# Float64 weights rounded in other steps, a piece apart, and mostly beside the first batch's MLP

## The chip, the cores and the metric

The kernel runs on one core of a Trainium2 chip. The metric is device time in microseconds (us) of one execution. Executions of one kernel agree within about 0.3%. The engines are named as the profile names them: PE (TensorE, matrix products), PEld (its weight loads), DVE (VectorE), ACT (ScalarE), POOL (GpSimd), SP (SyncE, which only issues transfers here).

## The reference, cut to what matters

```python
# attention: 8 batches, 12 heads, 448 positions, 64 per head, float32
q_n, k_n = rmsnorm(q, g_q), rmsnorm(k, g_k)
attn = softmax(q_n @ k_n.T / 8)
x = (attn @ v)  # (8, 12, 448, 64), rearranged to 3584 tokens x 768
# MLP: the weights w_in (768 x 2048) and w_out (2048 x 768) come as float64
h = x @ w_in
out = ((h - np.tanh(h)) @ w_out).astype(np.float32)
```

The weights arrive as float64. The kernel loads them as pairs of 32-bit words (low and high) and builds float32 values from them. This building is called rounding here. It works on 64 pieces of 128 partitions x 384 values, 32 for w_in and 32 for w_out.

## The kernel before: the parts that matter

The work is cut into slots, one for each pair of heads, 48 in all. In slot s the kernel loads for s+3, normalises and transposes for s+2, computes scores and exponentials for s+1, and the product with v for s. Between these parts lie four gaps, in which pieces of the previous batch's MLP and roundings are emitted. In the traces below an engine that waits for one instruction holds up those emitted after it.

```python
def round_weight(nc, pool, raw, dst, n):          # all of one piece at once
    lo, hi = raw[:, :, 0], raw[:, :, 1]
    ...
    nc.vector.tensor_scalar(out=ex, in0=hi, scalar1=0x7FF00000, ..., op0=ALU.bitwise_and)        # exponent
    nc.gpsimd.tensor_scalar(out=exf, in0=ex, scalar1=8.0, scalar2=-896.0 * 2**23, op0=ALU.mult, op1=ALU.add)
    nc.gpsimd.tensor_scalar(out=ex, in0=exf, scalar1=255.0 * 2**23, scalar2=0.0, op0=ALU.min, op1=ALU.max)
    nc.vector.tensor_scalar(out=man, in0=hi, ..., op0=ALU.bitwise_and, op1=ALU.bitwise_or)       # mantissa
    nc.vector.scalar_tensor_tensor(out=manf, in0=lo.bitcast(U32), scalar=2.0**-32, in1=man, ...)
    nc.vector.scalar_tensor_tensor(out=ex, in0=hi, scalar=-(2**31), in1=ex, ...)                 # sign
    nc.scalar.mul(manf, manf, 2.0**-20)
    nc.gpsimd.tensor_tensor(out=dst, in0=manf, in1=exf, op=ALU.mult)

# slot(s):  norm(s+2): squares (POOL), sums (DVE), pow (POOL), n = q * rr (DVE)
#           scores(s+1, 0); gap(0); values(s): av, dn (PE), rd = 1/dn and xT = av*rd (DVE); gap(1)
#           scores(s+1, 1); gap(2); turn(s+2): transposes (PE), kT (DVE), qT (ACT); gap(3)
for s in range(-2, NP + NP // 2):                 # NP = 6 slots a batch
    # slots -2..5: 32 pieces of w_in, no MLP; slots 6..8: 32 pieces of w_out beside the first MLP
    ...
    weight(n + 3, n)                              # load 3 ahead into 3 raw buffers, round
```

The hidden layer of the MLP accumulates in two PSUM tiles: `th` (tanh, ACT) and `gT` (h - th, DVE) must have read a tile before PE can fill it again.

## Time and profile before

| | before |
|---|---|
| time, median of the runs with the changed kernel | 1763.6 us |
| stage 1: slots 0 to 4, attention only, a slot | 23.4 us |
| the same, mean of slots 0 to 5 by their first scores: (190.9 - 46.5) / 6 | 24.1 us |
| stage 2: slots 6, 7 and 8, first MLP begins | 42.9, 50.6, 51.0 us |
| from slot 9 on, PE always busy, a slot | 32.55 us |

A slot's time runs from the start of its product with v (av) to that of the next. Where one time is given for all of stage 1, it is the mean of six slots between first scores, as in the second row.

Busy times by stage, from the table of windows. The columns are: window and its length in us; busy us (and instructions) of PE, PEld, DVE, ACT and POOL; granted PE clock; DMA share; GB/s.

```profile
29.80:194.60 164.80, 89.69 (x361) 37.22 (x359) 106.37 (x163) 47.63 (x92) 96.76 (x106) 0.71 0.33 97
194.60:346.30 151.70, 118.80 (x346) 53.78 (x347) 113.09 (x175) 36.37 (x72) 83.47 (x104) 0.90 0.33 95
346.30:1759.00 1412.70, 1407.38 (x4792) 709.81 (x4792) 473.28 (x558) 261.95 (x482) 194.31 (x122) 1.00 0.09 26
```

The third line is PE-bound: 1407 of 1413 us busy at full clock. The first two are not bound by any one engine. These 316 us are where a change to the rounding can act. The first two lines begin at 29.8 and 194.6 us: the first scores of slot 0 came at 46.5 us and those of slot 6 at 190.9.

### The profile page before, as it was taken

How to read it: one execution, taken by the hardware profiler on the slowest of the kernel's cores; microseconds unless marked ns; L12 is line 12 of the kernel's file. 1: busy time of each engine (PE TensorE's matmuls, PEld its weight loads, DVE VectorE, ACT ScalarE, POOL GpSimd, SP SyncE). 2: the span in 40 equal slices, each digit the busy share in tenths (PEclk: the TensorE clock that was granted, in tenths of full speed). 3: DMA queues.
4: the chain of work that ended last, by engine and by line, in shares of the span. 5: the costliest groups of instructions: out<-in, count | busy, mean ns of one | idle time of the engine just before them, and what ended most of it. 6: DMA issues, size and time to landing. Idle time of an engine off the chain costs nothing.

```text
span 1759.5 us, 14368 instructions
## 1 busy us (share of the span) xinstructions
PE 1621.6 (92%) x5512; PEld 804.2 (46%) x5512; DVE 705.2 (40%) x923; ACT 351.2 (20%) x653; POOL 388.9 (22%) x350
## 2 busy tenths in 40 slices
PE   1566767899999999999999999999999999999998
PEld 1222333355445554455445554454455544455555
DVE  4666777743443333433442333332442333421100
ACT  1232222212121122112121122112221112210100
POOL 5565555521112112112111112111121111100000
PEclk9776888999999999999999999999999999999999
DMA  4333332301001101011001110010001110000000
GB/s 119 103 91 102 90 100 83 93 29 40 22 16 40 35 25 27 21 34 35 21 16 40 35 35 16 26 40 26 21 16 40 35 36 16 10 14 9 0 19 20
DMA packets 93585, 70.23 MB, mean 40 GB/s; under 512 B 48452, under 2 KB 89412, under 8 KB 93508
## 3 DMA queue, kind: packets, MB, share of 16 engines
q1 hardware_dynamic: 93184, 69.23, 13.6%
q8 instruction: 45, 0.74, 0.2%
q14 instruction: 32, 0.26, 0.0%
q10 hardware_dynamic: 324, 0.00, 0.0%
HBM read 58.20 MB, written 11.01 MB: 39 GB/s over the span
## 4 chain that ended last, share of the span: by engine, by line
PE 80%; POOL 8%; DVE 8%; issue 2%; ACT 1%; DMA 0%; SPq 0%; POOLq 0%; ACTq 0%; DVEq 0%
PE mm L286 34%; PE mm L259 29%; PE sc L199 7%; PE av L228 7%; POOL w_exp L47 2%; POOL rr L161 2%; DVE w_exp L56 2%; POOL w_exp L44 2%; PE dn L237 2%; DVE rd L242 1%; POOL n L157 1%; DVE rr L158 1%; POOL w_out L60 1%; PE sc L177 1%; PE sc L182 1%
## 5 line engine op out<-in xcount | busy, mean ns | idle before, releaser
L259 PE MATMUL mm<-xT,w_in 128*128 128x448 f32 x1536 | 609.7, 551 | 20.7 <-DVE gT L266 20.6
L286 PE MATMUL mm<-w_out,gT 128*128 128x384 f32 x1536 | 513.6, 490 | 0.0
L259 PEld LDWEIGHTS mm<-xT,w_in 128*128 128x128 f32 x1536 | 289.1, 193 | 325.9 <-issue 315.3
L286 PEld LDWEIGHTS mm<-w_out,gT 128*128 128x128 f32 x1536 | 286.1, 190 | 222.4 <-issue 36.8
L204 ACT ACTIVATE p<-sc,rr 112x448 f32<-112x448 f32 x384 | 212.4, 633 | 382.7 <-PE sc L199 382.6
L242 DVE RECIPROCAL rd<-dn 128x448 f32<-128x448 f32 x48 | 141.9, 2955 | 249.6 <-PE dn L237 249.6
L157 POOL TENSOR_TENSOR n<-k_nat 112x512 f32<-112x512 f32 x48 | 49.9, 1039 | 765.5 <-PE sc L182 758.2
L199 PE MATMUL sc<-qT,kT 64*112 64x448 f32 x768 | 183.6, 599 | 33.0 <-DVE kT L179 33.0
L228 PE MATMUL av<-p,v_nat 112*64 112x448 f32 x768 | 159.7, 559 | 0.0
L266 DVE TENSOR_TENSOR gT<-mm,th 128x448 f32<-128x448 f32 x128 | 79.5, 621 | 200.0 <-ACT th L265 200.0
L265 ACT ACTIVATE th<-mm 128x448 f32<-128x448 f32 x128 | 69.6, 544 | 448.5 <-PE mm L259 433.1
L218 DVE TENSOR_TENSOR sum<-p 112x896 f32<-112x896 f32 x84 | 91.7, 1092 | 151.9 <-ACT p L204 147.5
L161 POOL TENSOR_TENSOR rr<-rr,neg_half 112x16 f32<-112x16 f32 x48 | 139.3, 2902 | 50.7 <-DVE rr L160 49.6
L199 PEld LDWEIGHTS sc<-qT,kT 64*112 64x112 f32 x768 | 66.6, 184 | 130.8 <-issue 91.6
L158 DVE TENSOR_REDUCE rr<-n 112x8 f32<-112x512 f32 x96 | 65.6, 683 | 92.9 <-POOL n L157 92.9
L228 PEld LDWEIGHTS av<-p,v_nat 112*64 112x64 f32 x768 | 52.2, 141 | 103.4 <-issue 102.3
L177 PE MATMUL sc<-ident,k_nat 112*128 112x112 f32 x192 | 30.1, 284 | 71.6 <-ACT p L204 63.1
L164 DVE TENSOR_TENSOR n<-q_nat,rr 112x512 f32<-112x512 f32 x48 | 36.4, 759 | 147.0 <-POOL rr L161 147.0
L286 PE MATMUL mm<-w_out,g_rest 128*128 128x384 f32 x256 | 85.4, 489 | 0.0
L157 POOL TENSOR_TENSOR n<-q_nat 112x512 f32<-112x512 f32 x48 | 49.9, 1039 | 141.0 <-DVE rr L158 141.0
L59 ACT ACTIVATE w_man<-w_man 128x384 f32<-128x384 f32 x64 | 33.4, 522 | 218.7 <-DVE w_man L53 218.6
L177 PEld LDWEIGHTS sc<-ident,k_nat 112*128 112x128 f32 x192 | 24.0, 153 | 92.5 <-ACT p L204 70.4
(37 smaller groups left out, 679.7 us busy)
## 6 DMA issues: line engine op xcount, KB each, us to landing
w_raw<-in_moe_w_in_dram SPq DMA_DIRECT2D x32, 384.0 KB, 3.4
w_raw<-in_moe_w_out_dram SPq DMA_DIRECT2D x32, 384.0 KB, 3.1
k_nat<-in_k_dram SPq DMA_DIRECT2D x96, 112.0 KB, 3.1
q_nat<-in_q_dram SPq DMA_DIRECT2D x48, 224.0 KB, 3.1
v_nat<-in_v_dram SPq DMA_DIRECT2D x48, 224.0 KB, 2.6
out_dram<-o_sb SPq DMA_DIRECT2D x48, 192.0 KB, 1.9
out_dram<-o_sb SPq DMA_DIRECT2D x16, 96.0 KB, 2.2
gcol<-in_g_q_dram ACTq DMA_DIRECT2D x2, 0.2 KB, 2.3
```

Of the source, the lines that this page charges most:

```text
L157: nc.gpsimd.tensor_tensor(out=sq, in0=rows, in1=rows, op=ALU.mult)
L158: nc.vector.reduce_sum(rr[:, i], sq, axis=AX.X)
L161: nc.gpsimd.tensor_tensor(out=rr2, in0=rr2, in1=neg_half, op=ALU.pow)
L177: nc.tensor.transpose(tk[:, c * CP : (c + 1) * CP], kn[:, c].rearrange("p h d -> p (h d)"), ident[:CP, :CP])
L199: nc.tensor.matmul(sc[:CP, :S], lhsT=kT[r, c * CP : (c + 1) * CP], rhs=qT[r, :], start=True, stop=True)
L204: nc.scalar.activation(p[:, h, i, :], tiles[h][:CP, :S], AF.Exp, scale=rr[:, 0, 2 * c + h : 2 * c + h + 1])
L218: nc.vector.tensor_tensor(out=u, in0=a, in1=z, op=ALU.add)
L228: nc.tensor.matmul(av[h * D : (h + 1) * D, :S], lhsT=v_nat[:, h, c, :], rhs=p[:, h, c % 2, :], start=(c == 0), stop=(c == NCH - 1),)
L242: nc.vector.reciprocal(rd, dn[:, :S])
L259: nc.tensor.matmul(hps[:, :S], lhsT=w_in_sb[f][:, c, :], rhs=xT[b, c], start=(c == 0), stop=(c == CD - 1))
L266: nc.vector.tensor_tensor(out=g[:, f, :], in0=hps[:, :S], in1=th, op=ALU.subtract)
L286: nc.tensor.matmul(ops[:, :HALF], lhsT=lhs[:, f, :], rhs=w_out_sb[f][:, d], start=(f == 0), stop=(f == CF - 1),)
```

## The change

The intent: fewer steps for a piece, no engine that waits inside a piece (the second half of a piece is emitted after the first half of the next), and less rounding ahead of the first MLP. The raw words of w_in are loaded into the memory that later holds w_out, so up to 14 can be loaded ahead. n moves behind rd and xT on DVE, kT from DVE to ACT.

The new steps of a piece: ACT scales the absolute value of the high word, read as a float, and scales the low word; POOL limits the first of these to a range (called the clamp here). Then DVE shifts the bits into place and puts the sign back, and POOL adds the low word's share to the bits.

```diff
+HI_MIN, HI_MAX = 2.0**-31, 1.875 - 2.0**-23
+def round_weight_a(nc, raw, dst):
+    lo, hi = raw[:, :, 0], raw[:, :, 1]
+    nc.scalar.activation(dst, hi.bitcast(F32), AF.Abs, scale=2.0**-16)
+    nc.scalar.mul(lo, lo.bitcast(U32), 2.0**-29)
+    nc.gpsimd.tensor_scalar(out=dst, in0=dst, scalar1=HI_MIN, scalar2=HI_MAX, op0=ALU.max, op1=ALU.min)
+def round_weight_b(nc, raw, dst):
+    lo, hi = raw[:, :, 0], raw[:, :, 1]
+    bits = dst.bitcast(I32)
+    nc.vector.tensor_scalar(out=bits, in0=bits, scalar1=4, scalar2=1, op0=ALU.logical_shift_left, op1=ALU.logical_shift_right)
+    nc.vector.scalar_tensor_tensor(out=bits, in0=hi, scalar=-(2**31), in1=bits, op0=ALU.bitwise_and, op1=ALU.bitwise_or)
+    nc.gpsimd.tensor_tensor(out=bits, in0=bits, in1=lo, op=ALU.add)
...
+    EARLY = 20
+        if n < 2 * CF:                       # w_in: staged where w_out will be
+            raw = w_out_sb[n % CF].bitcast(I32).rearrange("p (f w) -> p f w", w=2)
...
+        else:                                # w_out: three raw buffers, as before
+            raw = wp.tile([P, HALF, 2], I32, name="w_raw")
...
+    def weight(to):
+        for n in range(done[1], min(to, 4 * CF)):
+            round_weight_a(nc, raws[n], weight_dst(n)[2])
+            if n:
+                round_weight_b(nc, raws.pop(n - 1), weight_dst(n - 1)[2])
+            done[1] = n + 1
+            while done[0] < min(max(min(n + 14, 2 * CF + 3), n + 3), 4 * CF):
+                weight_load(done[0])
+                done[0] += 1
...
-        nc.vector.tensor_scalar(out=kT, in0=tk[:, :S], scalar1=g_col, ...)
+        nc.scalar.mul(kT, tk[:, :S], g_col)
...
         for f in range(CF):                  # hidden layer of batch 0: pieces 20 to 47
+            if b == 0:
+                weight(EARLY + (3 * CF - EARLY) * (f + 1) // CF)
...
+                if b == 0 and n == 0:        # first column half of its output: pieces 48 to 63
+                    weight(3 * CF + CF * (t * CF + f + 1) // (FULL * CF))
...
         gap(1)
+        if has(2):
+            norm_q(s + 2)                    # n, here in place of the end of norm
...
+    for s in range(-2, NP):                  # 20 pieces in slots -2 to 5
+        slot(s, lambda j: weight(EARLY * (4 * (s + 2) + j + 1) // (4 * (NP + 2))))
```

More of the change, by code (lines that the diff above doesn't have):

```diff
@@ L60, in round_weight @@
     nc.gpsimd.tensor_tensor(out=dst, in0=manf, in1=exf, op=ALU.mult)
+HI_MIN, HI_MAX = 2.0**-31, 1.875 - 2.0**-23
[7 more added lines that the diff above has]
+    bits = dst.bitcast(I32)
+    nc.vector.tensor_scalar(
+        out=bits, in0=bits, scalar1=4, scalar2=1, op0=ALU.logical_shift_left, op1=ALU.logical_shift_right
+    )
+    nc.vector.scalar_tensor_tensor(
+        out=bits, in0=hi, scalar=-(2**31), in1=bits, op0=ALU.bitwise_and, op1=ALU.bitwise_or
+    )
+    nc.gpsimd.tensor_tensor(out=bits, in0=bits, in1=lo, op=ALU.add)
 def bounded_path(tc, ctx, q, k, v, moe_w_in, moe_w_out, out, g_col, ident, ones, neg_half):
@@ L94, in bounded_path @@
     gp = pool("gp", bufs=1)
+    op = pool("op", bufs=3)
+    wp_stack = ctx.enter_context(ExitStack())
+    wp = wp_stack.enter_context(tc.tile_pool(name="wp", bufs=3))
     ps_s = pool("ps_s", bufs=4, space=PSUM)
@@ L122, in bounded_path, with weight_dst, weight_load @@
     raws = {}
-    def weight_load(wp, n):
-        f, i = n // 2 % CF, n % 2
-        raw = raws[n] = wp.tile([P, HALF, 2], I32, name="w_raw", bufs=3)
+    def weight_dst(n):
         if n < 2 * CF:
+            f, i = n // 2, n % 2
+            return f, i, w_in_sb[f].rearrange("p c f -> p (c f)")[:, i * HALF : (i + 1) * HALF]
+        i, f = (n - 2 * CF) // CF, n % CF
+        return f, i, w_out_sb[f][:, i * HALF : (i + 1) * HALF]
+    def weight_load(n):
+        f, i, _ = weight_dst(n)
+        if n < 2 * CF:
+            raw = w_out_sb[n % CF].bitcast(I32).rearrange("p (f w) -> p f w", w=2)
             rows = w_in_words[i * HALF : (i + 1) * HALF, f * 2 * P : (f + 1) * 2 * P]
@@ L138, in weight_load @@
             )
-    def weight_round(wp, n):
-        f, i = n // 2 % CF, n % 2
-        if n < 2 * CF:
-            dst = w_in_sb[f].rearrange("p c f -> p (c f)")[:, i * HALF : (i + 1) * HALF]
-        else:
-            dst = w_out_sb[f][:, i * HALF : (i + 1) * HALF]
-        round_weight(nc, wp, raws.pop(n), dst, HALF)
+        raws[n] = raw
+    done = [0, 0]
+    def weight(to):
[7 more added lines that the diff above has]
+                done[0] += 1
+        if done[1] == 4 * CF and raws:
+            round_weight_b(nc, raws.pop(4 * CF - 1), weight_dst(4 * CF - 1)[2])
     normed, turned, probs, sums, xT = {}, {}, {}, {}, {}
@@ L161, in norm, with norm_q @@
         nc.gpsimd.tensor_tensor(out=rr2, in0=rr2, in1=neg_half, op=ALU.pow)
+        normed[s] = rr
+    def norm_q(s):
+        rr = normed[s]
         t = loaded.pop(("q", s))
@@ L178, in turn @@
         kT = qkp.tile([P, S], F32, name="kT")
-        nc.vector.tensor_scalar(out=kT, in0=tk[:, :S], scalar1=g_col, scalar2=None, op0=ALU.mult)
+        nc.scalar.mul(kT, tk[:, :S], g_col)
         tq = ps_s.tile([P, 512], F32, name="sc")
@@ L270, in hidden @@
         late["g"] = g
-    def project(b):
-        op = late["op"]
-        g = late.pop("g")
-        if b % 2 == 0:
-            late["rest"] = op.tile([P, CF, P], F32, name="g_rest", bufs=1)
-        o = (b % 2) * REST
-        nc.gpsimd.tensor_copy(out=late["rest"][:, :, o : o + REST], in_=g[:, :, FULL * P :])
-        for t in range(FULL + b % 2):
-            lhs = g[:, :, t * P : (t + 1) * P] if t < FULL else late["rest"]
-            for n in range(2):
-                d = slice(n * HALF, (n + 1) * HALF)
-                ops = ps_m.tile([P, 512], F32, name="mm")
-                for f in range(CF):
-                    nc.tensor.matmul(
-                        ops[:, :HALF], lhsT=lhs[:, f, :], rhs=w_out_sb[f][:, d],
-                        start=(f == 0), stop=(f == CF - 1),
-                    )
-                    if f < CF - 1:
-                        yield 4 * HALF / ENGINE_NS
-                o_sb = op.tile([P, HALF], F32, name="o_sb", bufs=3)
-                if n == 0:
-                    nc.scalar.copy(out=o_sb, in_=ops[:, :HALF])
-                else:
-                    nc.vector.tensor_copy(out=o_sb, in_=ops[:, :HALF])
-                if t < FULL:
-                    r0 = b * S + t * P
-                    nc.sync.dma_start(out=out[r0 : r0 + P, d], in_=o_sb)
-                else:
-                    for i in range(2):
-                        r0 = (b - 1 + i) * S + FULL * P
-                        nc.sync.dma_start(out=out[r0 : r0 + REST, d], in_=o_sb[i * REST : (i + 1) * REST])
-                yield 4 * HALF / ENGINE_NS
@@ new lines, in rest @@
+    def rest(b):
+        if b == 0:
+            late["op"] = pool("late", bufs=1)
+        if b % 2 == 0:
+            late["rest"] = late["op"].tile([P, CF, P], F32, name="g_rest")
+        o = (b % 2) * REST
+        nc.gpsimd.tensor_copy(out=late["rest"][:, :, o : o + REST], in_=late["g"][:, :, FULL * P :])
+    def project(b):
+        g = late["g"]
+        units = [(t, n) for t in range(FULL + b % 2) for n in range(2)]
+        if b == 0:
+            units.sort(key=lambda u: u[1])
+        else:
+            rest(b)
+        for t, n in units:
+            lhs = g[:, :, t * P : (t + 1) * P] if t < FULL else late["rest"]
+            d = slice(n * HALF, (n + 1) * HALF)
+            if b == 0 and (t, n) == (0, 1):
+                wp_stack.close()
+                rest(b)
+            ops = ps_m.tile([P, 512], F32, name="mm")
+            for f in range(CF):
+                if b == 0 and n == 0:
+                    weight(3 * CF + CF * (t * CF + f + 1) // (FULL * CF))
+                nc.tensor.matmul(
+                    ops[:, :HALF], lhsT=lhs[:, f, :], rhs=w_out_sb[f][:, d],
+                    start=(f == 0), stop=(f == CF - 1),
+                )
+                if f < CF - 1:
+                    yield 4 * HALF / ENGINE_NS
+            o_sb = op.tile([P, HALF], F32, name="o_sb")
+            if n == 0:
+                nc.scalar.copy(out=o_sb, in_=ops[:, :HALF])
+            else:
+                nc.vector.tensor_copy(out=o_sb, in_=ops[:, :HALF])
+            if t < FULL:
+                r0 = b * S + t * P
+                nc.sync.dma_start(out=out[r0 : r0 + P, d], in_=o_sb)
+            else:
+                for i in range(2):
+                    r0 = (b - 1 + i) * S + FULL * P
+                    nc.sync.dma_start(out=out[r0 : r0 + REST, d], in_=o_sb[i * REST : (i + 1) * REST])
+            yield 4 * HALF / ENGINE_NS
@@ L347, in slot @@
         gap(3)
-    with tc.tile_pool(name="wp", bufs=2) as wp:
-        done = [0, 0]
-        def weight(n_load, n_round):
-            while done[0] < min(n_load, 4 * CF):
-                weight_load(wp, done[0])
-                done[0] += 1
-                while done[1] < min(n_round, done[0] - 2):
-                    weight_round(wp, done[1])
-                    done[1] += 1
-            while done[1] < min(n_round, done[0]):
-                weight_round(wp, done[1])
-                done[1] += 1
-        load(0, "kqv")
-        weight(3, 0)
-        for s in range(-2, NP + NP // 2):
-            def gap(j, s=s):
-                if s < NP:
-                    n = 2 * CF * (4 * (s + 2) + j + 1) // (4 * (NP + 2))
-                else:
-                    n = 2 * CF + 2 * CF * (4 * (s - NP) + j + 1) // (2 * NP)
-                    run(per_slot / 4)
-                weight(n + 3, n)
-            slot(s, gap)
-    late["op"] = pool("op", bufs=3)
-    for s in range(NP + NP // 2, NS):
+    load(0, "kqv")
+    for n in range(4):
+        weight_load(n)
+    done[0] = 4
+    for s in range(-2, NP):
+        slot(s, lambda j: weight(EARLY * (4 * (s + 2) + j + 1) // (4 * (NP + 2))))
+    for s in range(NP, NS):
         slot(s, lambda j: run(per_slot / 4))
```

## The prediction

> **What bounds the kernel now.** I read the forty slices of the page first, then busy times by stage, then the timeline of one slot of each stage, then the waits of the stage that held most.
>
> ```profile
> PE   1566767899999999999999999999999999999998
> PEclk9776888999999999999999999999999999999999
> ```
>
> From slice 9 on (one slice is 44 us) PE is full at full clock; nothing the change does to VectorE, ScalarE or GpSimd can shorten that part. The time to win is in the first eight slices. The kernel works in slots of one head pair: slots -2 to 5 hold attention of the first batch and round w_in (32 pieces, 4 a slot); slots 6 to 8 start that batch's MLP and round w_out (32 pieces, 10.7 a slot); from slot 9 no rounding is left. One window of each kind:
>
> ```profile
> 97.00:120.40 23.40, 13.62 (x58) 5.56 (x56) 15.23 (x23) 6.82 (x14) 13.84 (x16) 0.72 0.33 98
> 243.60:295.80 52.20, 38.85 (x115) 16.97 (x116) 38.81 (x60) 12.74 (x27) 29.31 (x38) 0.90 0.34 97
> 378.80:411.35 32.55, 32.55 (x121) 17.18 (x122) 10.83 (x12) 5.90 (x11) 4.98 (x3) 1.00 0.13 40
> ```
>
> Columns: window, length, then busy us of PE, weight load, DVE, ACT, POOL, granted clock, DMA share, GB/s. A slot takes 23.4 us in stage 1, 52.2 in stage 2 and 32.55 where PE is the bound. No engine is full in the first two: DVE reaches 15.2 of 23.4 and 38.8 of 52.2. So it is a chain across engines, not a busy engine. The timeline of one piece in stage 2 shows it:
>
> ```profile
> 256.98 0.35 DVE L43 TENSOR_SCALAR w_exp<-w_raw 128x384 int32<-128x384 int32 x1
> 257.22 1.00 POOL L60 TENSOR_TENSOR w_out<-w_man,w_exp 128x384 f32<-128x384 f32 x1 [0.74 <-DVE w_exp L56]
> 257.25 1.18 DVE L50 TENSOR_SCALAR w_man<-w_raw 128x384 int32<-128x384 int32 x1
> 258.30 0.51 POOL L44 TENSOR_SCALAR w_exp<-w_exp 128x384 f32<-128x384 int32 x1
> 258.46 0.75 DVE L53 SCALAR_TENSOR_TENSOR w_man<-w_raw,w_man 128x384 f32<-128x384 uint32 x1
> 258.89 0.69 POOL L47 TENSOR_SCALAR w_exp<-w_exp 128x384 int32<-128x384 f32 x1
> 259.31 0.52 ACT L59 ACTIVATE w_man<-w_man 128x384 f32<-128x384 f32 x1 [2.58 <-DVE w_man L53]
> 259.61 0.56 DVE L56 SCALAR_TENSOR_TENSOR w_exp<-w_raw,w_exp 128x384 int32<-128x384 int32 x1 [0.40 <-POOL w_exp L47]
> ```
>
> DVE and POOL hand one piece to and fro, and it costs DVE 3.1 us (L43 to the next L43), which is 33 us for 10.7 pieces. Other DVE work is about 13.3 us in such a slot (rd 2.95, xT 0.96, four sums 3.4, two reductions 1.4, n 0.7, kT 0.7, 5.3 gT of 0.6), and n waits for POOL's pow and the reductions for POOL (some 6 us). 33 + 13 + 6 = 52: the slot's length. PE then waits for the tanh result to leave PSUM, behind that queue:
>
> ```profile
> PE mm L259 <- DVE gT L266: 20.6, 6, 6.3
> ```
>
> (waits of stage 2: total us, times, longest). Stage 1 has the same chain with the norm (POOL square, DVE sum, twice; pow; n) inside it.
>
> **What the Trainium skill says.**
> "SBUF — State Buffer", section Who interferes with whom: a DVE instruction in a two-port mode and a GpSimd instruction exclude each other for their whole length. The trace agrees for the tensor_scalar (L50 takes 0.35 us alone, 1.18 when it meets L60's 1.00). The page says so of two-input DVE operations too; L53 over L47 above is only slowed (0.75 against 0.56), so I count the first as a block and the second not.
> "TensorE: Matmul & The Clock Gate", section What's actually happening: after an idle window of about 3.4 us the clock is halved until a busy one. The trace: eight score matmuls take 1.76 us warm, but 3.33 at 285.7 us behind an idle gap of only 2.72.
> "ScalarE: Activation LUTs", section What ACT_TABLE_LOAD costs: 186 ns + 0.833 ns per element with immediates, 506 ns at 384; L59 takes 522.
> "GPSIMD Engine Reference", section 4.1 Engine selection: an add with all operands of one 32-bit integer type is exact there. It gives no time for it; I take L60's 1.00 us, also two inputs of 384.
>
> **The change, part by part.**
> Rounding. Before, a piece costs DVE 0.41 + 0.71 + 0.74 + 0.56 = 2.42 us, POOL 0.53 + 0.68 + 1.00 = 2.21, ACT 0.52 (mean durations of its rows). After: ACT two activations, 1.04; POOL one tensor_scalar (0.51) and one add (1.00), 1.51; DVE one tensor_scalar (0.35) and one two-input operation (0.56, issued 0.3 apart), about 0.8 alone and, with a wait behind a running POOL operation, 1.5 estimated in dense stretches. As the second half belongs to the piece before, no engine waits inside a piece.
> Placement. Stage 1 rounds 20 pieces (2.5 a slot) in place of 32; stage 2 rounds 28 (9.3 a slot) in place of 32; the last 16 go beside the first output units of slots 9 and 10, which need only the other column half. No piece comes late: output f of the hidden layer needs 2(f+1) pieces and 20 + 1.75(f+1) are rounded.
> Staging in w_out's place gives 14 loads of lookahead. It removes waits of the DMA queue, which cost nothing now, and makes a burst of 10 loads at 11 us.
> norm_q: n goes behind rd and xT on DVE, so DVE no longer sits 3 us behind pow, but n is then chained to PE. kT (0.68) goes from DVE to ACT.
>
> Stage 1 after. The rounding leaves the chain and a new loop sets the slot: scores half 0, av and dn on PE, rd and xT on DVE, n, transposes of q, qT on ACT, next scores. Warm: 1.76 + 3.2 + 3.1 = 8.0 (PE), 0.1, rd and xT 3.77 (start of L242 to the next DVE start), 0.4 for a piece in half of the slots, n 0.7, transposes 0.6, qT 0.53, handovers 0.2: 14.3 us. With the PE cold at its start, as now (scores 3.33, av 4.65, transposes 1.0), 17.6. PE's longest idle gap in it is about 2.8 us, where it sits seven now: sometimes cold, I take 16.5. POOL's own chain (last add, two squares, pow) ends about 10 us after the n before, so it is not the bound. ACT (8 exponentials 5.1, kT and qT 1.2, rounding 2.6) is at 9. The two first slots have no values; the norm chain of 7.7 us (8.55 to 16.2 in the trace) plus transposes and copies puts the first scores of slot 0 at about 27.5 us. Slot 6's scores then start at 27.5 + 6 x 16.5 = 126.5 us; before, at 190.9. Gain 64.4.
>
> Stage 2 after. DVE: 12.6 + 9.3 x 1.5 + some 3 of waits for the norm = 29.6 of 32.55; POOL 5.0 + 14.1 = 19; ACT 8 exponentials, 5.3 tanh, copies and 9.7 of rounding = 19. PE becomes the bound again, but DVE is close behind and the output of the hidden layer has only two PSUM buffers, so PE will lose a few us when gT stands behind rd and a piece. I put the slot at 36. First scores of slot 6 to its av take 10.8 now and stay; av of slot 9 comes 10.8 + 3 x 36 = 118.8 us after them, now 155.4 (346.3 - 190.9). Gain 36.6.
>
> Slots 9 and 10 carry 16 pieces, without tanh and gT: some 2 us lost. From there all is as before.
>
> Sum: 1762.8 - 64.4 - 36.6 + 2 = 1664 us, 5.6% less.
>
> **Rivals.**
> DVE stays the bound of stage 2. Its 29.6 of 32.55 rests on my 1.5 us a piece; if the port lock makes it 2.4 (0.51 + 0.35 + 0.56 + 1.00, fully in turn), the slot is 12.6 + 22 + 3, about 39 with PE's idle gaps, and the time 1674. For it: L50's 1.18. Against it: L53 overlaps.
> The loop of stage 1 keeps PE warm or cold throughout: 14.3 gives 1651, 17.6 gives 1671. For cold: the 2.72 us gap. For warm: the gap is less than half of today's.
> The burst of loads holds back k and q of the third head pair. The present highest, 119 GB/s at 0.43 share, puts the limit at an estimated 277 GB/s; 7.3 MB are queued ahead, 26 us, so they land about 32 us, just as needed. A miss costs 2 to 5 us, once.
> The rounding is hidden anyway: then nothing changes. Stage 2's 52 against 32.55 us speaks against it.
> PE stalls of stage 2 vanish: 32.55 a slot, 1654.
>
> **Range and chances.** The rivals that look likely span 1642 to 1690 when two come together. Even one stage's gain alone (36 us) passes 2% (35 us), so slower is all but excluded.
>
> **What would show it.** Slots of stage 1 at 14 to 18 us between starts of rd, with rd released by dn, and n directly behind xT. The first hidden matmul (L259 now, at 194.2 us) at about 130. Slots 6 to 8 at 33 to 39 us with PE's waits for gT under 4 us a slot. Steady slots still 32.55. The rounding's DVE tensor_scalar between 0.35 and 1.2 us. I am wrong if the integer add or the strided activation takes far over 1.00 or 0.52 us, if ACT, now with kT and two activations a piece, holds back exponentials, or if PE waits for weights at a batch's start.

## The result, and the profile after

The changed kernel takes 1690.05 us (1688.23 to 1690.59), the kernel before 1763.6. The ratio is 0.9583, 95% interval 0.9566 to 0.96. All ratios here are the mean time of one kernel's fast runs over that of the other's of the same rounds, so they aren't quite the ratio of the quoted medians. The kernel is 4.2% faster, where 5.6% was predicted. The time lies 26 us above the predicted one and just outside the range, whose end was 1690.

The forty slices of the page, now of 42 us each:

```profile
PE   5788988899999999999999999999999999999998
PEclk9788999899999999999999999999999999999999
```

PE is full from the ninth slice on in both kernels (now from about 337 us, before from about 352 us), and fuller than before in each of the first seven. In the eighth slice (295 to 337 us) PE shows an 8 still; the surprise lies close to there. The stages, in the same columns as before, with slots 9 and 10 as a stage of their own:

```profile
30.00:131.30 101.30, 79.15 (x336) 30.53 (x336) 55.83 (x69) 47.20 (x92) 70.95 (x49) 0.80 0.46 123
131.30:253.00 121.70, 111.85 (x352) 51.27 (x352) 82.38 (x108) 53.33 (x109) 92.22 (x69) 0.97 0.23 66
253.00:338.20 85.20, 72.19 (x239) 36.27 (x238) 48.95 (x59) 27.32 (x55) 58.60 (x43) 0.92 0.36 103
```

The windows start at the first scores of slot 0, the first scores of slot 6, and av of slots 9 and 11. Set beside the prediction:

| | predicted | measured | off |
|---|---|---|---|
| first scores of slot 6 | 126.5 us | 131.3 | +4.8 |
| from there to av of slot 9 | 118.8 | 121.7 | +2.9 |
| slots 9 and 10 beyond 2 x 32.55 | 2 | 20.1 | +18.1 |

The sum of the last column is 25.8 us; the profiled run (1688.2 us) lies 24 above the prediction, so these terms hold the whole miss. One term carries most of it: the two slots in which the last 16 pieces are rounded. Of its 20.1 us PE sat idle for 13.0 (85.20 - 72.19); the other 7.1 are matmuls that took longer, the granted clock being 0.92 over these slots. DVE lost its load there as intended. Beside PE, POOL is the busy one: 92 of 122 us in stage 2 and 59 of 85 in stage 3.

Stage 1, from the chain that ended last (start, us, what; the view leaves out the shortest pieces). This is one turn of the predicted loop, from scores to scores:

```profile
97.25 3.33 PE sc L251 x8
100.58 3.92 PE av L280 x16
104.50 3.03 PE dn L289 x16
107.56 2.97 DVE rd L294
110.55 0.96 DVE xT L296
112.20 0.69 DVE n L216
113.03 0.99 PE sc L234 x4
114.69 3.33 PE sc L251 x8
```

The eight score matmuls take 3.33 us: the granted clock is 0.50 there, and at 1.00 they take 1.76. rd starts when dn is done, n comes behind xT, and the transposes of q follow at once. A slot takes (131.3 - 30.4) / 6 = 16.8 us; 16.5 was predicted.

Now the clamp of the changed kernel (L74, the tensor_scalar on POOL) by its own line; the three times are the shortest, the median and the longest in ns:

```profile
L74 POOL TENSOR_SCALAR w_in<-w_in x32: 1482/1493/1862, 15.0 to 185.0; 128x384 f32<-128x384 f32 x32
L74 POOL TENSOR_SCALAR w_out<-w_out x32: 1482/1491/1919, 187.6 to 314.8; 128x384 f32<-128x384 f32 x32
```

The prediction gave it 0.51 us. Its shortest is 1.48, and the 16 that ran with no DVE instruction beside them took 1.49 too. So it isn't held up by DVE: it is that long by itself. What this does in slot 9 is seen in the timeline (start, us, engine, line, tiles, and in brackets how long the engine sat idle before, and for what):

```profile
281.78 1.06 POOL L87 TENSOR_TENSOR w_out<-w_out,w_raw 128x384 int32<-128x384 int32 x1 [1.57 <-DVE w_out L84]
...
285.92 0.55 ACT L72 ACTIVATE w_out<-w_raw 128x384 f32<-128x384 f32 x1 [4.42 <-DMA w_raw<-in_moe_w_out_dram]
286.38 0.53 ACT L73 ACTIVATE w_raw<-w_raw 128x384 int32<-128x384 uint32 x1
286.56 1.49 POOL L74 TENSOR_SCALAR w_out<-w_out 128x384 f32<-128x384 f32 x1 [0.98 <-ACT w_out L72]
286.81 0.62 ACT L231 ACTIVATE kT<-sc,g_col 128x448 f32<-128x448 f32 x1
287.32 0.52 ACT L238 COPY qT<-sc 128x448 f32<-128x448 f32 x1
287.90 1.76 PE L251 MATMUL sc<-qT,kT 64*112 64x448 f32 x8 [3.19 <-ACT qT L238]
```

ACT sat idle for 4.42 us, waiting for raw words that had not landed. kT and qT were ready to run behind it (their transposes were done at 276.8 us), but ACT keeps its order, and PE then stood 3.19 us for qT. The load was late because one of the three raw buffers is free only when POOL's add (L87) of three pieces before has read it: that add, the first line here, ended at 282.84, the load was issued at 282.87 and landed at 285.90. The waits of the changed kernel from 130 to 335 us (total us, times, longest):

```profile
ACT w_out L72 <- DMA w_raw<-in_moe_w_out_dram: 72.8, 25, 8.0
...
PE mm L353 <- POOL w_out L87: 6.6, 5, 2.9
PE mm L313 <- DVE gT L320: 6.0, 2, 3.4
PE sc L251 <- ACT qT L238: 5.3, 3, 3.2
PE sc L229 <- ACT p L256: 3.9, 2, 3.2
```

PE waits for the weight itself, for qT and for the exponentials p. Only 6.0 us are the wait for gT that ruled before (20.6).

Two theories follow. Theory A: POOL's clamp is the cause, 1 us too long on 64 pieces. Theory B: the ring of three raw buffers (add, load, two activations, clamp, add) is the cause, and a faster clamp would only shift the wait. A third question is whether stage 1 is really bound by the loop shown.

### The profile page after: what moved, and what is told of

Its sections match the earlier page's. It is cut to its first block, busy times and chain, and to the rows that moved or that the text cites. A ratio compares the mean times of both kernels' runs of the same rounds, so it can differ in the third digit from the quotient of the medians.

```text
span 1686.4 us, 14244 instructions
## 1 busy us (share of the span) xinstructions
PE 1615.3 (96%) x5512; PEld 798.6 (47%) x5512; DVE 616.1 (37%) x747; ACT 405.3 (24%) x765; POOL 415.4 (25%) x286
## 3 DMA queue, kind: packets, MB, share of 16 engines
q1 hardware_dynamic: 93184, 69.23, 14.5%
## 4 chain that ended last, share of the span: by engine, by line
PE 85%; POOL 6%; DVE 4%; issue 3%; DMA 1%; ACT 1%; SPq 0%; ACTq 0%; POOLq 0%; DVEq 0%
PE mm L353 33%; PE mm L313 31%; PE sc L251 9%; PE av L280 8%; PE dn L289 3%; POOL w_out L74 2%; DVE rd L294 2%; POOL w_out L87 1%; PE sc L234 1%; POOL n L205 1%; DMA w_raw<-in_moe_w_out_dram 1%; PE sc L229 1%; POOL rr L209 1%; POOL w_in L87 1%; POOL w_in L74 1%
## 5 line engine op out<-in xcount | busy, mean ns | idle before, releaser
L313 PE MATMUL mm<-xT,w_in 128*128 128x448 f32 x1536 | 601.7, 545 | 7.7 <-DVE gT L320 6.0
L353 PE MATMUL mm<-w_out,gT 128*128 128x384 f32 x1536 | 519.9, 494 | 6.6 <-POOL w_out L87 6.6
L313 PEld LDWEIGHTS mm<-xT,w_in 128*128 128x128 f32 x1536 | 285.7, 190 | 307.5 <-issue 293.6
L353 PEld LDWEIGHTS mm<-w_out,gT 128*128 128x128 f32 x1536 | 287.7, 191 | 233.3 <-issue 38.7
L205 POOL TENSOR_TENSOR n<-k_nat 112x512 f32<-112x512 f32 x48 | 49.9, 1040 | 736.1 <-PE sc L234 729.2
L205 POOL TENSOR_TENSOR n<-q_nat 112x512 f32<-112x512 f32 x48 | 50.0, 1041 | 139.1 <-DVE rr L206 139.1
L363 DVE COPY o_sb<-mm 128x384 f32<-128x384 f32 x28 | 15.5, 554 | 153.2 <-PE mm L353 152.9
L353 PEld LDWEIGHTS mm<-w_out,g_rest 128*128 128x128 f32 x256 | 47.9, 190 | 35.6 <-issue 4.1
L333 POOL COPY g_rest<-gT 128x1024 f32<-128x1024 f32 x8 | 9.0, 1131 | 202.2 <-DVE gT L320 202.1
L361 ACT COPY o_sb<-mm 128x384 f32<-128x384 f32 x28 | 13.4, 478 | 188.2 <-PE mm L353 188.1
```

What stands on the lines that cost most here:

```text
L205: nc.gpsimd.tensor_tensor(out=sq, in0=rows, in1=rows, op=ALU.mult)
L313: nc.tensor.matmul(hps[:, :S], lhsT=w_in_sb[f][:, c, :], rhs=xT[b, c], start=(c == 0), stop=(c == CD - 1))
L353: nc.tensor.matmul(ops[:, :HALF], lhsT=lhs[:, f, :], rhs=w_out_sb[f][:, d], start=(f == 0), stop=(f == CF - 1),)
```

## The experiments

Each edit is to the changed kernel. All results were correct.

### The clamp's two operations swapped

```diff
-    ...(out=dst, in0=dst, scalar1=HI_MIN, scalar2=HI_MAX, op0=ALU.max, op1=ALU.min)
+    ...(out=dst, in0=dst, scalar1=HI_MAX, scalar2=HI_MIN, op0=ALU.min, op1=ALU.max)
```

> The clamp on GpSimd with its two operations in the other order (min, then max; the same values). The changed kernel's clamp takes 1.49 us at its median, where I had 0.51 from the old kernel's two tensor_scalars; one of those was min then max. Theory A (it is the order of the two operations that costs): the clamp falls to 0.5 to 0.7 us, slots 9 and 10 from 42.6 to 36 or less, the time from 1690 to 1665 to 1675. Theory B (float32 in and float32 out costs 1.49 us whatever the order): clamp and time unchanged, 1690 within 3.

Measured: 1666.4 us (ratio to before 0.945, interval 0.9434 to 0.9466). The clamp's line:

```profile
L74 POOL TENSOR_SCALAR w_out<-w_out x32: 502/507/1302, 181.9 to 296.6; 128x384 f32<-128x384 f32 x32
```

The same values in the other order take 0.51 us in place of 1.49, and the kernel gains 23.6 us. Slots 6 and 7 run at 33.0 and 32.7 us, PE's own pace. Slot 10 falls to 32.5. But slots 8 and 9 still take 38.5 each, where 36 or less was expected, and ACT's wait for loads is 59 us. So the clamp is a cause, and not the only one.

### The clamp on DVE

```diff
-    nc.gpsimd.tensor_scalar(out=dst, in0=dst, scalar1=HI_MIN, ...)
+    nc.vector.tensor_scalar(out=dst, in0=dst, scalar1=HI_MIN, ...)
```

> The clamp goes from GpSimd to VectorE, so GpSimd has only the integer add of about 1.0 us a piece and VectorE one tensor_scalar more, 0.35 us alone and 1.2 behind a GpSimd operation. If GpSimd's 1.49 us is what makes slots 9 and 10 long (42.6 us against the steady 32.6), they fall to 33 to 37 and the time to 1665 to 1675. If the three staging buffers set it (load 3.1 us, two activations 1.0, the rest), they stay at 40 or more and the time at 1683 or more.

Measured: 1680.1 us (0.952), between the two cases. Slots 6 and 7 take 32.7, but slots 8 to 10 take 38.6, 43.2 and 40.5, nearly as long as with the slow clamp on POOL (39.8, 42.6 and 42.6). The clamp itself is short (0.39 us mean), but now stands in DVE's queue behind rd and xT, and POOL's adds waited 55 us for DVE's second operation on w_out pieces, where it was 7 us:

```profile
POOL w_out L87 <- DVE w_out L84: 55.3, 20, 5.3
```

So POOL was freed, but a turn of the ring was not shortened, and slots 9 and 10 stayed above 40. This speaks for theory B there, but does not prove it, as the edit also loads DVE.

### Four raw buffers

```diff
-    op = pool("op", bufs=3)
+    op = pool("op", bufs=2)
-    ...tc.tile_pool(name="wp", bufs=3)
+    ...tc.tile_pool(name="wp", bufs=4)
-            while done[0] < min(max(min(n + 14, 2 * CF + 3), n + 3), 4 * CF):
+            while done[0] < min(max(min(n + 14, 2 * CF + 4), n + 4), 4 * CF):
```

> Four raw buffers in place of three and one load more ahead (the output staging goes from three buffers to two to make room, which should cost nothing). If the ring of three buffers is the bound of slots 9 and 10 (GpSimd frees a buffer, the load takes 3.1 us, ScalarE waits for it in order), these fall from 42.6 to about 37 us and the time to about 1680; ScalarE's wait for the w_out loads falls from 73 us to under 35. If GpSimd's busy time is the bound, all stay within 3 us of 1690, with the wait moved elsewhere.

Measured: 1678.66 us (0.9522), 11.4 us less than the changed kernel, with the slow clamp in place. ACT's wait for loads fell to 50.1 us, not to 35, and slots 8 to 10 take 37.3, 34.4 and 42.3. The ring is a part of the cause; with POOL this slow the wait came back in slot 10. (The edit also takes one of three buffers from the output's staging; no run separates this.)

### Swapped clamp and four raw buffers

> The clamp as min then max (0.5 us) and four raw buffers. With the clamp swapped alone the time was 1666.4 and slots 8 and 9 still took 38.5 us each, with ScalarE waiting 59 us for w_out loads. If the ring of buffers is what is left there, both fall to 33 to 35, the wait for loads to under 35 us, and the time to 1655 to 1661. If something else holds them (the add of GpSimd behind VectorE), the time stays within 3 of 1666.

Measured: 1654.96 us (0.9391, interval 0.9375 to 0.9406). Slot 9 of the changed kernel first, for comparison, then slot 9 of this one, then its wait for loads, in the columns of the earlier views:

```profile
253.00:295.60 42.60, 34.97 (x121) 17.97 (x120) 27.61 (x33) 14.56 (x30) 33.10 (x25) 0.96 0.46 127
```

```profile
240.20:272.80 32.60, 32.60 (x121) 17.21 (x120) 26.71 (x31) 16.50 (x34) 22.96 (x26) 1.00 0.61 166
```

```profile
ACT w_out L72 <- DMA w_raw<-in_moe_w_out_dram: 27.4, 15, 6.2
```

PE is busy for all of slot 9, and slots 6 to 10 all take 32.5 to 33.2 us. Clamp and ring together account for the whole excess there, and they add up: 23.6 + 11.4 = 35.0, and 1690.05 - 1654.96 = 35.1.

### n before rd and xT in the first slots

```diff
         if has(2):
             norm(s + 2)
+            if s < NP:
+                norm_q(s + 2)
...
-        if has(2):
+        if has(2) and s >= NP:
             norm_q(s + 2)
```

> In the first slots (up to 5) n is computed before rd and xT again, as in the kernel before; later slots keep the new order. Theory: stage 1's slot of 16.8 us is the loop scores, av, dn, rd, xT, n, transposes, qT; without rd and xT in it PE and ScalarE set the slot at 12.5 to 14.5 us and the time falls by 14 to 25, to 1665 to 1676. Rival (GpSimd's norm chain or ScalarE sets it): slots stay above 16 us and the time within 4 of 1690.

Measured: 1689.84 us (0.9582), no change; the slot is (128.7 - 30.7) / 6 = 16.3 us. Stage 1 ended 2.6 us earlier, and slot 6 took 41.5 us in place of 37.5. The rival held. The timeline shows what took the loop's place:

```profile
77.42 2.94 DVE L294 RECIPROCAL rd<-dn 128x448 f32<-128x448 f32 x1
...
81.59 0.56 DVE L84 SCALAR_TENSOR_TENSOR w_in<-w_out,w_in 128x384 int32<-128x384 int32 x1
...
82.23 1.06 POOL L87 TENSOR_TENSOR w_in<-w_in,w_out 128x384 int32<-128x384 int32 x1 [4.28 <-DVE w_in L84]
83.26 1.79 POOL L74 TENSOR_SCALAR w_in<-w_in 128x384 f32<-128x384 f32 x1
85.03 1.00 POOL L87 TENSOR_TENSOR w_in<-w_in,w_out 128x384 int32<-128x384 int32 x1
86.00 1.03 POOL L205 TENSOR_TENSOR n<-k_nat 112x512 f32<-112x512 f32 x1
```

DVE's part of a piece now stands behind rd and xT, POOL's add waits 4.28 us for it, and the next slot's norm (L205) comes only behind two adds and a clamp. As the timeline reads, a loop through DVE and POOL of nearly the same length had been lying under the one removed; the next run and the last one test this.

### The same with the swapped clamp

> Clamp as min then max, and in the first slots n before rd and xT. With the slow clamp this changed nothing, because VectorE's part of a piece then stood behind rd and xT and GpSimd's next norm behind that piece's clamp and add. With a clamp 1 us shorter, two of them in that chain, stage 1's slot should be 14.5 to 15.5 us in place of 16.9 and the time 1654 to 1661. If the chain is not GpSimd's, slots stay above 16.3 and the time within 4 of 1666.

Measured: 1662.61 us (0.943), 3.8 less than the swap alone: the slots of the first case, the time of the second. Stage 1's slot falls to 15.4 us, where it was 16.3 with n moved alone and 17.0 with the swap alone: so POOL's clamp was in the chain once n had moved. But slot 6 takes 38.6 us in place of 33.0 and gives half of the gain back; that the MLP now begins before the engines have caught up is the likely reason, not a tested one.

### All of w_in in the first slots, with the swapped clamp

```diff
-    EARLY = 20
+    EARLY = 32
```

> Clamp as min then max, and all 32 w_in pieces in the first slots in place of 20, so 16 pieces fall to slots 6 to 8 in place of 28. If stage 1 is the loop over rd, xT and n with room beside it, its slots grow by under 1 us (16.9 to 17.8), slot 8 falls from 38.5 to 33 to 36, and the time is 1660 to 1668. If stage 1 has no room, its slots grow by 1.5 us or more and the time is above 1672.

Measured: 1668.54 us (0.9461), within the noise of the 1666.4 with 20. Stage 1's slots take 17.3 us against 17.0, the first scores come 5.6 us later (35.2 against 29.6 us), and slots 8 to 10 take 33.2, 34.3 and 39.6: the wait moved from slots 8 and 9 to slot 10. It neither helps nor hurts.

### The old places for the rounding

```diff
-    EARLY = 20
+    EARLY = 32
-                weight(EARLY + (3 * CF - EARLY) * (f + 1) // CF)
+                weight(EARLY + (4 * CF - EARLY) * (f + 1) // CF)
```

> The new rounding with its 1.49 us clamp, in the old places: all 32 w_in pieces in slots -2 to 5, all 32 w_out pieces in slots 6 to 8, none beside the output units. If the new place is needed for the gain, the stage 2 slots rise to 45 or more and the time to 1715 or more. If the steps of the rounding give nearly all of it and the place next to nothing, stage 1 slots go to 17.5 to 19, stage 2 slots to 36 to 42, slots 9 and 10 fall to 32.6, and the time is 1675 to 1695.

Measured: 1696.48 us (0.9625), 6.4 more than the changed kernel, just outside the second case. Slots 6 to 8 take 43.3, 42.0 and 43.5 us, and slots 9 and 10 the steady 32.5. With the clamp as it is, the new place earns 6 of the 73.5 us.

### The norm's order and kT undone

```diff
             norm(s + 2)
+            norm_q(s + 2)
...
-        if has(2):
-            norm_q(s + 2)
...
-        nc.scalar.mul(kT, tk[:, :S], g_col)
+        nc.vector.tensor_scalar(out=kT, in0=tk[:, :S], scalar1=g_col, scalar2=None, op0=ALU.mult)
```

> The changed kernel with its two smaller parts undone: n right behind pow on VectorE in every slot, and kT on VectorE. If they matter where the rounding runs beside the MLP (VectorE stands 3 us behind pow, gT behind it), slots 6 to 10 grow by 1 to 3 us each and the time is 1694 to 1702. If they are hidden anyway, 1690 within 3.

Measured: 1689.71 us (0.9583). These two parts do nothing for the time. DVE does stand 3.0 us behind pow again in each slot (18.2 us for six), but PE's wait for gT is 6.6 us against 6.0.

### Which form of the clamp is slow

The clamp in other forms: max alone, min alone, max twice, min twice. The results stayed correct in all four, so the output does not need either limit on these weights.

> The clamp reduced to its first half, max with the small constant, on GpSimd (the upper clamp never acts on these weights, so the result may stay correct). The swap showed that min then max takes 0.5 us where max then min takes 1.49. If max as a first or only operation is slow, this takes 1 us or more. If only the pair in that order is slow, it takes 0.4 to 0.6 us and the time is near 1666.

> The clamp as a single min. So far: max then min 1.49 us, max alone 1.17, min then max 0.51. If a max in first place is what is slow, min alone takes 0.5 us or less. If every operation that is not one fast pair takes the slow way, min alone takes about 1.2 us too.

> The clamp as max then max, both with the small constant. If a max in first place is slow, 1.2 us or more; if only certain pairs are fast and this is one, 0.5 us.

> The clamp as min then min, both with the large constant. If min in first place is fast, 0.5 us. If only the pair min then max is fast, about 1.5 us.

The clamp's line in each, in this order:

```profile
L74 POOL TENSOR_SCALAR w_in<-w_in x32: 1162/1172/1542, 15.3 to 186.4; 128x384 f32<-128x384 f32 x32
```

```profile
L74 POOL TENSOR_SCALAR w_in<-w_in x32: 1157/1170/1542, 15.6 to 186.4; 128x384 f32<-128x384 f32 x32
```

```profile
L74 POOL TENSOR_SCALAR w_in<-w_in x32: 1487/1497/1862, 15.3 to 184.7; 128x384 f32<-128x384 f32 x32
```

```profile
L74 POOL TENSOR_SCALAR w_in<-w_in x32: 1488/1499/1864, 15.2 to 185.1; 128x384 f32<-128x384 f32 x32
```

It isn't max in first place. A single min costs as much as a single max (1.17 us), and two of a kind as much as max then min (1.49 to 1.50). Min then max is the exception at 0.51. Even less work, a single operation, is slower than this pair. The kernel before used the fast forms by chance or by care: min then max and mult then add, 0.51 us each at the shortest (0.69 and 0.54 at the median). Why the pair is fast no run here shows. The times (1683.86, 1682.05, 1687.89 and 1686.36 us) fit: between 1666 and 1690, the two shorter clamps below the two longer ones.

### A version that beats both

The three edits that helped together:

> The three edits that helped together: clamp as min then max, four raw buffers, n before rd in the first slots. If they add up: 1655 less the 4 to 10 us that the last one gave, 1645 to 1651, with stage 1 slots of 15.4 to 15.8 us and the later slots at 33. If the earlier start only makes the rounding late for the MLP, as it seemed in the run without the fourth buffer (slot 6 took 38.6), the time stays above 1652.

Measured: 1651.91 us (0.9371). Stage 1's slot is 15.4 us, slots 7 to 10 take 32.5 to 33.2, slot 6 38.7. They add up only in part, as feared: slot 6 gives back what the earlier start won.

The last kernel also rounds all pieces of a first slot in gap(0), ahead of rd on DVE:

```diff
-        slot(s, lambda j: weight(EARLY * (4 * (s + 2) + j + 1) // (4 * (NP + 2))))
+        slot(s, lambda j: weight(EARLY * (s + 3) // (NP + 2) if j == 0 else 0))
```

> As the one before, and in the first slots all the slot's pieces are rounded ahead of rd, so GpSimd's adds no longer wait for VectorE behind rd and xT and the next norm can start. If that wait is what holds stage 1 now, its slots fall from 15.7 to 12.5 to 14 us and the time to 1630 to 1640. If PE, half the time at the lower clock, or ScalarE is next, slots stay at 14.5 or more and the time above 1641.

Measured: 1641.05 us (0.9309, interval 0.9293 to 0.9325), 6.9% faster than before and 49 us faster than the change. The slots of stage 1 average 14.5 us, from 12.8 to 17.0, just on the edge between the two cases. One of the short ones, at its start:

```profile
86.90 1.76 PE L251 MATMUL sc<-qT,kT 64*112 64x448 f32 x8 [1.40 <-ACT qT L238]
```

From the third of these slots on the scores take 1.76 us where they took 3.33, as the granted clock (third column from the end) stays full. The second and the third slot:

```profile
43.90:60.90 17.00, 14.38 (x58) 5.27 (x58) 12.25 (x14) 8.12 (x16) 11.91 (x13) 0.75 0.47 118
60.90:74.10 13.20, 10.80 (x58) 4.28 (x58) 8.88 (x11) 7.16 (x14) 8.36 (x8) 1.00 0.39 114
```

POOL's longest wait for DVE's second operation between 50 and 115 us fell from 5.3 us in the run before to 1.5. So POOL's wait behind rd and xT was one bound of stage 1, and removing it also brought the clock back. The two longest slots, 16.0 and 17.0 us, are the first two, in which the clock is still halved for a part; what holds the fifth at 15.2 was not separated.

## Why the prediction was right or wrong

**The bound, the stages and what could be won: right.** The gain lies wholly before slot 11; the steady slots are 32.5 to 32.9 us as before.

**Stage 1: right in mechanism and nearly in size.** The chain after shows the predicted loop link by link, with the cold scores. The slot is 16.8 us for 16.5. The first scores came at 30.4 us for 27.5. Both together are the +4.8. The estimate of 1.5 us of DVE for a piece came out at 1.41 (0.67 + 0.75, the means). What the prediction missed is how near the next bound lay: it put POOL's own chain at "about 10 us", with neither a clamp nor a wait for DVE in it. With n moved ahead, these made it as long as the loop.

**"POOL one tensor_scalar (0.51)": this is the step that failed.** The clamp takes 1.49 us. The prediction took the shortest time of the kernel before's two tensor_scalars on POOL for any tensor_scalar of that size. Those happened to be forms that the chip runs three times as fast. The prediction named the danger for the integer add and the activation ("far over 1.00 or 0.52 us"), which came in at 1.01 and 0.56 at the median, and not for the clamp. Undone, it is worth 23.6 us, and the time would then have been 1666.4 against a predicted 1664.

**"Some 2 us lost" in slots 9 and 10: wrong by 18 us, and only partly for the clamp.** With the fast clamp those two slots still lost 5.9 us (38.5 + 32.5 - 65.1) and slot 8 lost another 6. The prediction treated the lookahead of 14 loads as if it held for all pieces and dismissed the waits of the DMA queue as costing nothing. For w_out there are still three buffers, and ACT waits for their loads in its own order, ahead of exponentials, kT and qT. The prediction did list "if ACT ... holds back exponentials" among what would make it wrong, without a number. The fourth buffer took 11.4 us off, with either clamp.

**That 1664 nearly equals the run with the fast clamp is partly luck.** In that run the three terms of the table are off by +5.4, -4.4 and +3.9 us. Stage 2 was predicted at 36 us a slot for DVE near its bound. With clamp and ring mended all its slots run at 33, PE's pace: the rival "PE stalls of stage 2 vanish" was right, and DVE was never the bound there. So an estimate 9.7 us too long for stage 2 (118.8 predicted, 109.1 measured with both mended) stood against the missing ring.

**norm_q and kT: no effect either way**, where the prediction counted the end of DVE's 3 us wait as part of stage 2's gain. **Placement: 6 us.** So the gain of 73 us is the new rounding and its staging; this is argued from these two runs, as no kernel had the new steps alone with everything else old.

**The burst of loads** was listed as a rival worth 2 to 5 us once. The first scores were 2.9 us late; no run separates the burst's part in it.

## What to carry to other kernels

Take the duration of an instruction only from the very same form, its operations and their order included: two equal clamps differed threefold, and swapping the operations won 23.6 us. Where an engine does the first step on data that a ring of few buffers brings in, work out the ring's full turn divided by its buffers as a bound of its own: here a fourth buffer won 11.4 us, and everything queued behind that step had paid for the wait. When a loop is predicted as the bound, compute the next one under it with its waits, before counting on the gain from opening the first.

## What the Trainium skill lacked or had wrong

- "GPSIMD Engine Reference", section 4.1 Engine selection, calls one-input work "roughly line-rate". For 128 x 384 float32, min then max takes 0.51 us, but a single max or min 1.17 and max then min, max twice or min twice 1.49 to 1.50. No page gives times for these forms or says that the order of the two operations matters.
- The same section states that the 32-bit integer add is exact but gives no time: 1.01 us at the median for 128 x 384, with one input at a stride of two words, as long as the float32 multiply of the kernel before (1.00).
- "SBUF — State Buffer", section Who interferes with whom, has a DVE operation with two SBUF inputs contend with any GpSimd operation that reads SBUF, as an exclusive lock. The trace of the changed kernel shows degrees: DVE's scalar_tensor_tensor (L84) takes 0.56 us alone, 0.74 to 0.75 beside the clamp or the pow (20 of 29 times, 0.56 in the others), and 1.25 whenever it meets the add (12 times). The section makes no difference between them.
- "TensorE: Matmul & The Clock Gate", section What's actually happening, ties the half clock to an idle window of about 3.4 us. Here no such gap is needed: the scores ran at the half rate (3.33 us) in the slots 1 to 5 of the changed kernel, whose longest gap was 2.6 to 3.3 us, and at 90.4 us of the run with three edits behind no gap over 1.24; in the last run they kept the full rate (1.76) though one gap was 3.01. What fits is PE's busy share. The clock record of the 17 traces changes only at steps of 3.41 us. Cut at these steps, up to 360 us, the clock was halved 160 times, each time after a step in which PE was busy for less than 0.50 of it (only 8 steps under 0.50 did not halve it), and it came back only after steps of 0.83 or more.
- "ScalarE: Activation LUTs", section What ACT_TABLE_LOAD costs, gives an estimate of 506 ns by its formula for 384 elements. The activations that read every second 32-bit word took 0.55 to 0.56 us at the median, the contiguous one of the kernel before 0.52. The formula has no term for a strided input; whether the stride makes the difference no run separates.
